# Row-sum reciprocals taken once per half of an attention unit, and two more weight chunks converted ahead of the FFN

## The chip, the cores and the metric

The kernel runs on one core of a Trainium2 chip. The metric is the device time of one execution in microseconds (us). Five engines work side by side, each through its own instructions in order: PE (matmul), DVE (vector), ACT (activations, copies), POOL (GpSimd), and SP, which issues all DMAs here. Before the change the median of three runs is 726.29 us (726.19 to 726.36).

## The reference

An attention with a position bias is followed by a two-layer feed-forward block (FFN). 4 batches, 8 heads, 576 positions, head width 64; FFN width 2048; all in float32.

```python
def _attn_ref(q, k, v, w1, b1, w2):
    scores = scale * np.matmul(q, k.transpose(0, 1, 3, 2))
    psi_rel = np.log1p(np.abs(pos[:, None] - pos[None, :]))
    psi_i = np.log1p(np.maximum(pos[:, None], 1.0))
    bias = np.maximum((psi_rel / psi_i)[..., None] @ w1 + b1, 0.0) @ w2
    scores = scores + bias.transpose(2, 0, 1)[None]
    attn = np.exp(scores - np.max(scores, axis=-1, keepdims=True))
    attn = attn / (np.sum(attn, axis=-1, keepdims=True) + 1e-09)
    return np.matmul(attn, v)

def _moe_ref(x, w_in, w_out):
    h = x @ w_in
    return np.maximum(0.01 * h, h) @ w_out
```

The second function is applied to the first one's result, as 2304 tokens of 512.

## The kernel before, in words

**Three stages follow one another.** First the position bias is made and written to DRAM (`gen_*`, to some 56 us). Then come 16 attention units of one head pair and one batch each. Then the FFN runs over five token blocks (`BLOCKS`: four of 512 and one of 256 tokens).

**A unit** has nine tiles in the order `KINDS`: A0, B0, A1, B1, M, A2, B2, A3, B3. A and B are the two heads, the digit is a group of 128 query rows, and M holds the last 64 rows of both heads. A0 to B1 with half of M make the half g=0, the rest g=1. The main loop calls `step(n)` for each tile number n. One step issues, in this order: the score matmuls of tile n (L230, into one of two PSUM buffers `ps_s`) and its softmax start on DVE (L252: bias added, scaled, row minimum taken); the reciprocal work `recip` of tile n-1 (L265, L266 on DVE, L269 on POOL, which spreads the reciprocals over a 128-wide tile `rb`); what is left of earlier outputs (L360; then `pv_exit`: L344, L345 and L348); the transposes of tile n-3 (`transposes`, L295, L298, L299, L314, L315 on PE, with the copies into the tile `PT` on ACT, L302 and L311, and DVE, L305 and L317); the product with v (`pv`, L335), twice per unit; and last the exponential on ACT (L260). "Step 6" below is the step whose n is six tiles into a unit; pv of half 0 is issued in step 0 of the next unit, pv of half 1 in step 4 of it. A score matmul needs its `ps_s` buffer back, so it waits for the softmax start two tiles earlier.

Every row sum is turned into its reciprocal, spread by POOL, transposed by PE beside the last 64 columns of the probabilities, and copied on into row 9 of `PT`, where `pv_exit` multiplies by it. Units 1, 5, 9 and 13 do more in `pv_exit`: there the tokens of block 0 are also split into a high part and a low rest (L344, L345, L360).

**Work laid between.** In steps 0 and 4, from unit 2 on, the loop pops two operations of `early_ops`: the conversion of the FFN weights. A chunk m has two halves (`wi`, `wo`). Each half takes one ACT operation (`w_abs`, L400), four on DVE (`w_bits`, L407, L409, L411, L413) and then the split into two parts (`w_hi` on ACT, L419; `w_lo` on DVE, L423). In attention the bits of chunks 0 to 4 are made; only chunk 0 is split as well. In the same steps DVE casts the q and k of the next unit (L192, L197), and POOL makes their low parts (L204, L207).

**The FFN's first block** carries the rest of the conversion. It has 16 rows, one for each chunk m: `ffn1` (12 matmuls, L441), the activations on ACT (`ffn_act`, L449 and L450, both out of one buffer), the rest `gl` on DVE (`ffn_lo`, L456) and `ffn2` of the row two before (12 matmuls, L467 to L469). A list `todo` holds the conversion operations with a cost each; `work(budget)` pops them until the budget is used, twice in a row:

```python
                work(2.6)
                ffn_act(n, m)
                work(2.6)
                ffn_lo()
```

So what `todo` puts on ACT and DVE stands ahead of that row's activations and of its `gl`. `ffn2` of row 0 adds up in the two `ps_s` buffers that `ffn1` of rows 0 and 1 filled, so its second half needs the activations of row 1 done. Each engine keeps to the written order.

Of the kernel before, what the change touches and what calls it, by code (L numbers as in the profile page):

```python
# [8 lines left out]
F32 = mybir.dt.float32  # L9
# [26 lines left out]
def attention_ffn(ctx: ExitStack, tc: tile.TileContext, qt, kt, vm, vt, wi, wo, cst, out):  # L36
# [199 lines left out]
    def softmax_a(n):  # L236
        u, kind = tile_id(n)
        hp = u // B
        bt = bias[hp, "M"][:] if kind == "M" else bias[hp, kind[1]][:, 0 if kind[0] == "A" else 1, :]
        col = 1 if kind[0] == "B" else 0  # L240
        if col == 0:
            mx_t[n] = ap.tile([128, 2], F32, tag="mx", name="mx", bufs=6)
            sm_t[n] = ap.tile([128, 4], F32, tag="sm", name="sm", bufs=6)
        else:
            mx_t[n], sm_t[n] = mx_t[n - 1], sm_t[n - 1]
# [8 lines left out]
        ex_q.append((p, i, sm_t[n][:, col:col + 1]))  # L254

# [18 lines left out]
    pv_q = []

    def pt_tile(u, g):
        PT[u, g] = ap.tile([128, 10, HS], F32, tag="PT", name="PT", bufs=2)

    def halves(t):
        return t[:].rearrange("p (a c) -> p a c", a=2)  # L280

    def transposes(n, at):
        u, kind = tile_id(n)
        p = pp.pop(n)
        p0 = S + 64 if kind[0] == "B" else 0
        if kind == "A0":
            pt_tile(u, 0)
            tails[u, 0] = pstile("o")
        elif kind == "M":
            pt_tile(u, 1)  # L290
            pv_ps[u, 0] = pstile("o")
            tails[u, 1] = pstile("o")
# [18 lines left out]
        nc.scalar.copy(out=PT[u, g][:, 0:8, c].rearrange("p (j h) c -> p j h c", h=2)[:, :, h, :], in_=t0[:].rearrange("p (j c) -> p j c", j=4))  # L311
        if h == 1:
            tl = halves(tails[u, g])
            nc.tensor.transpose(tl[:, 0, c], p[:, 512:640], ident[:])  # L314
            nc.tensor.transpose(tl[:, 1, c], rb_t.pop(n)[:], ident[:])  # L315
            if i2 == 1:
                nc.vector.tensor_copy(PT[u, g][:, 8:10, 0:256], tl)  # L317
                if g == 1:
                    pv_q.append((at, u, 1))
# [159 lines left out]
    with tc.manual_schedule():  # L479
# [7 lines left out]
        for n in range(NTILE + LAG + 6):  # L487
# [138 lines left out]
```

## Time and profile before

| what | value |
|---|---|
| median of three runs | 726.29 us |
| the profiled execution | 725.89 us, with a span of 723.7 us from its first to its last instruction |
| PE busy | 703.4 us (97%) |
| DVE busy | 394.2 us (54%) |
| ACT busy | 365.7 us (51%) |
| POOL busy | 127.0 us (18%) |
| mean granted TensorE clock | 1.000 |

A matmul's record overlaps the next one's, so PE's busy share says little. What a stage loses on PE is read from the time between equal points of the work, and from rows that carry a wait in square brackets: its length and who ended it.

### The profile page before, as it was taken

The numbers are of one execution on the slowest core, as the hardware profiler recorded it, in microseconds if no ns is written. First come the engines' busy times: TensorE is split into PE (matmuls) and PEld (weight loads), VectorE is DVE, ScalarE is ACT, GpSimd is POOL, SyncE is SP. The second block draws the span as 40 slices with busy tenths as digits, with TensorE's granted clock in tenths as the row PEclk, the third lists the DMA queues.
The fourth block names the chain that finished last, engine by engine and source line by source line (L and its number), as shares of the span: only waits on it lengthen the run. The fifth ranks groups of instructions, "written<-read, shape, count | busy, mean of one in ns | idle before, by whom it ended". The sixth has DMA issues, their size and how long they took to land.

```text
span 723.7 us, 11398 instructions
## 1 busy us (share of the span) xinstructions
PE 703.4 (97%) x4192; PEld 556.7 (77%) x4192; DVE 394.2 (54%) x1012; ACT 365.7 (51%) x808; POOL 127.0 (18%) x167
## 2 busy tenths in 40 slices
PE   6899999999999999998999999999999999999998
PEld 2347788778877887776777888888888888888996
DVE  7997789789888889759998211112111221112111
ACT  7797777777868677764555231132221231122221
POOL 2104545445544444300000000000000000000000
PEclk9999999999999999999999999999999999999999
DMA  9798848537626960103552010000100010000100
GB/s 222 241 314 244 224 109 242 129 88 216 188 69 164 249 172 18 59 1 120 175 175 83 1 58 1 1 0 1 58 1 1 0 59 1 0 1 0 59 1 30
DMA packets 30263, 68.26 MB, mean 94 GB/s; under 512 B 8192, under 2 KB 8320, under 8 KB 30208
## 3 DMA queue, kind: packets, MB, share of 16 engines
q1 hardware_dynamic: 30208, 67.54, 32.9%
q8 instruction: 33, 0.54, 0.3%
q14 instruction: 22, 0.18, 0.1%
HBM read 51.92 MB, written 15.61 MB: 93 GB/s over the span
## 4 chain that ended last, share of the span: by engine, by line
PE 80%; DVE 16%; issue 1%; DMA 1%; ACT 1%; SPq 0%; DVEq 0%
PE ps_o L441 11%; PE ps_t L441 11%; PE ps_o L335 10%; PE ps_s L230 10%; PE ps_s L469 8%; PE ps_s L467 8%; PE ps_s L468 8%; PE ps_t L295 7%; DVE p L252 2%; PE ps_o L123 2%; DVE tmp L411 2%; PE ps_t L123 2%; DVE tmp L413 2%; DVE r L112 2%; DVE wol L423 1%
## 5 line engine op out<-in xcount | busy, mean ns | idle before, releaser
L456 DVE TENSOR_TENSOR gl<-g,gh 128x512 fp32r<-128x512 f32 (+1 forms) x80 | 51.0, 638 | 263.9 <-ACT g L450 263.9
L230 PE MATMUL ps_s<-ks,qs 128*128 128x288 f32 x640 | 120.2, 314 | 3.1 <-DVE mx L252 3.1
L469 PE MATMUL ps_s<-woh,gl 128*128 128x512 f32 x288 | 112.9, 392 | 1.9 <-DVE gl L456 1.9
L467 PE MATMUL ps_s<-woh,gh 128*128 128x512 f32 x288 | 112.5, 390 | 1.6 <-ACT g L450 1.6
L468 PE MATMUL ps_s<-wol,gh 128*128 128x512 f32 x288 | 112.3, 390 | 0.0
L252 DVE CUSTOM_DVE_ANT_0 p<-ps_s,bias 128x576 f32<-128x576 f32 x128 | 95.0, 751 | 24.3 <-PE ps_s L230 23.6
L260 ACT ACTIVATE p<-p,mx 128x576 f32<-128x576 f32 x128 | 99.9, 780 | 11.3 <-DVE mx L252 10.4
L230 PEld LDWEIGHTS ps_s<-ks,qs 128*128 128x128 f32 x640 | 89.4, 189 | 18.8 <-DVE mx L252 5.0
L311 ACT COPY PT<-ps_t 128x512 f32<-128x512 f32 x128 | 73.7, 576 | 37.5 <-PE ps_t L295 37.5
L449 ACT ACTIVATE gh<-ps_o 128x512 fp32r<-128x512 f32 (+1 forms) x39 | 21.5, 552 | 124.4 <-PE ps_o L441 124.4
L295 PE MATMUL ps_t<-ident,p 128*128 128x128 f32 x512 | 76.9, 273 | 0.9 <-ACT PT L311 0.8
L449 ACT ACTIVATE gh<-ps_t 128x512 fp32r<-128x512 f32 (+1 forms) x39 | 21.5, 552 | 111.1 <-PE ps_t L441 111.0
L335 PE MATMUL ps_o<-PT,v 128*64 128x288 f32 x512 | 69.2, 412 | 0.0
L469 PEld LDWEIGHTS ps_s<-woh,gl 128*128 128x128 f32 x288 | 54.0, 188 | 16.2 <-DVE gl L456 5.0
L467 PEld LDWEIGHTS ps_s<-woh,gh 128*128 128x128 f32 x288 | 54.2, 188 | 12.6 <-ACT g L450 2.0
L295 PEld LDWEIGHTS ps_t<-ident,p 128*128 128x128 f32 x512 | 61.7, 140 | 2.7 <-ACT PT L311 1.8
L468 PEld LDWEIGHTS ps_s<-wol,gh 128*128 128x128 f32 x288 | 54.2, 188 | 10.6
L441 PE MATMUL ps_t<-xh,wil 128*128 128x512 f32 (+1 forms) x156 | 57.3, 367 | 0.0
L441 PE MATMUL ps_o<-xh,wil 128*128 128x512 f32 (+1 forms) x156 | 57.3, 367 | 0.0
L441 PE MATMUL ps_t<-xl,wih 128*128 128x512 f32 (+1 forms) x156 | 57.3, 367 | 0.0
L441 PE MATMUL ps_o<-xl,wih 128*128 128x512 f32 (+1 forms) x156 | 57.3, 367 | 0.0
L441 PE MATMUL ps_o<-xh,wih 128*128 128x512 f32 (+1 forms) x156 | 57.3, 367 | 0.0
(98 smaller groups left out, 1114.5 us busy)
## 6 DMA issues: line engine op xcount, KB each, us to landing
raw<-kt SPq DMA_DIRECT2D x32, 304.0 KB, 5.8
raw<-qt SPq DMA_DIRECT2D x32, 288.0 KB, 5.2
raw<-wi SPq DMA_DIRECT2D x16, 512.0 KB, 3.6
raw<-wo SPq DMA_DIRECT2D x16, 512.0 KB, 3.6
scr<-x SPq DMA_DIRECT2D x21, 295.5 KB, 4.0
bias<-scr SPq DMA_DIRECT2D x16, 288.0 KB, 5.3
out<-x SPq DMA_DIRECT2D x18, 256.0 KB, 2.1
v<-vm SPq DMA_DIRECT2D x16, 256.0 KB, 4.1
```

The source lines that it names most:

```text
L230: nc.tensor.matmul(s_[:, S0 + HS * hh:S0 + HS * hh + HS], qs[:, c0:c0 + 128], ks[:, k0 + HS * hh:k0 + HS * hh + HS], start=(j == 0), stop= ...
L252: nc.vector.tensor_tensor_reduce(out=p, in0=s_[:, S0:S0 + S], in1=bt, scale=-0.125, scalar=3.4e38, op0=ALU.add, op1=ALU.min, accum_out=i)
L260: nc.scalar.activation(out=p, in_=p, func=AF.Exp, bias=i, scale=-1.0, accum_out=sm)
L295: nc.tensor.transpose(t0[:, 128 * jb:128 * jb + 128], p[:, p0 + 128 * jb:p0 + 128 * jb + 128], ident[:])
L311: nc.scalar.copy(out=PT[u, g][:, 0:8, c].rearrange("p (j h) c -> p j h c", h=2)[:, :, h, :], in_=t0[:].rearrange("p (j c) -> p j c", j=4))
L335: nc.tensor.matmul(o[64 * h:64 * h + 64, 0:HS], l, r, start=(jb == 0), stop=(jb == 4))
L441: nc.tensor.matmul(h_[:, :N], w, x[:, :N], start=(j == 0), stop=(j == len(mms) - 1))
L449: nc.scalar.activation(out=gh[:, :N], in_=h_[:, :N], func=AF.Prelu, alpha=0.01)
L456: nc.vector.tensor_sub(gl[:, :N], g[:, :N], gh[:, :N].bitcast(F32))
L467: nc.tensor.matmul(o, gh[:, c], wt[m][2][:], start=(m == 0), stop=False)
L468: nc.tensor.matmul(o, gh[:, c], wt[m][3][:], start=False, stop=False)
L469: nc.tensor.matmul(o, gl[:, c], wt[m][2][:], start=False, stop=(m == MF - 1))
```

## The change

One tile of row sums serves a unit's half: four sums for g=1, five for g=0 with M. `recip` runs after M and after B3 alone, twice a unit instead of five times. POOL spreads four reciprocals over 256 columns in one copy and, after M, a fifth over 128. PE transposes the 256 columns in two pieces (`turn_rb`), in the step of M for half 0 and in that of B3 for half 1; the count of transposes stays. `PT` is one tile for all units, with both halves in it. With that M's copies become one on ACT and two on DVE, which were two and four. The PSUM tile that took the tails takes the product with v as well. Seven chunks' bits (`EARLY`) are made in attention instead of five, three operations at a time instead of two, with four 128x512 buffers for chunks 5 and 6. In the FFN `work` gets 2.1 instead of 2.6.

```diff
+EARLY = 7
+    tmp_x = {(m, i): xp.tile([128, DM], F32, name=f"y{m}{i}") for m in range(5, EARLY) for i in range(2)}
+    PT = ap.tile([128, 2, 10, HS], F32, name="PT")
...
+        g, sc = int(KINDS.index(kind) > 4), 4 if kind == "M" else 2 * (int(kind[1]) % 2) + col
+        if kind in ("A0", "A2"):
+            sm_t[u, g] = ap.tile([128, 12], F32, tag="sm", name="sm", bufs=3)
...
     def recip(n):
-        w = 2 if tile_id(n)[1][0] == "B" else 1
-        sm = sm_t[n]
+        u, kind = tile_id(n)
+        g = int(kind != "M")
+        sm, w = sm_t.pop((u, g)), 4 if g else 5
         nc.vector.tensor_scalar_add(sm[:, 0:w], sm[:, 0:w], 1e-9)
-        nc.vector.reciprocal(sm[:, 2:2 + w], sm[:, 0:w])
-        rb = rb_t[n] = ap.tile([128, 128], F32, tag="rb", name="rb", bufs=3)
-        one = sm[:, 2:2 + w].rearrange("p (h o) -> p h o", o=1).to_broadcast([128, w, 128 // w])
-        nc.gpsimd.tensor_copy(rb[:].rearrange("p (h c) -> p h c", h=w), one)
-        if w == 1:
+        nc.vector.reciprocal(sm[:, 6:6 + w], sm[:, 0:w])
+        rb = rb_t[u, g] = ap.tile([128, 384], F32, tag="rb", name="rb", bufs=2)
+        one = sm[:, 6:10].rearrange("p (h o) -> p h o", o=1).to_broadcast([128, 4, 64])
+        nc.gpsimd.tensor_copy(rb[:, 0:256].rearrange("p (h c) -> p h c", h=4), one)
+        if g == 0:
+            nc.gpsimd.tensor_copy(rb[:, 256:384], sm[:, 10:11].to_broadcast([128, 128]))
             nc.gpsimd.tensor_copy(pp[n][:, S:S + 64], pp[n][:, S - 64:S])
...
+    def turn_rb(u, g, rb):
+        for i in range(2):
+            nc.tensor.transpose(outs[u, g][:, 256 + 128 * i:384 + 128 * i], rb[:, 128 * i:128 * i + 128], ident[:])
+        nc.vector.tensor_copy(PT[:, g, 8:10, 0:256], halves(outs[u, g]))
...
-            for g in range(2):
-                nc.scalar.copy(out=PT[u, g][:, 0:8, 256:288].rearrange("p (j h) c -> p j h c", h=2), in_=src[:, :, :, g, :])
-                for h in range(2):
-                    r = slice(64 * h, 64 * h + 64)
-                    nc.vector.tensor_copy(PT[u, g][r, 8:10, 256:288], halves(tl)[r, :, 64 * h + 32 * g:64 * h + 32 * g + 32])
+            nc.scalar.copy(out=PT[:, :, 0:8, 256:288], in_=t0[:].rearrange("p (j g c) -> p g j c", j=8, g=2))
+            for h in range(2):
+                r, c = slice(64 * h, 64 * h + 64), slice(64 * h, 64 * h + 64)
+                nc.vector.tensor_copy(PT[r, :, 8:10, 256:288], halves(tl)[r, :, c].rearrange("p a (g c) -> p g a c", g=2))
+            turn_rb(u, 0, rb)
             pv_q.append((at, u, 0))
...
-        if 0 <= n - 1 < NTILE and KINDS[(n - 1) % 9][0] != "A":
+        if 0 <= n - 1 < NTILE and KINDS[(n - 1) % 9] in ("M", "B3"):
             recip(n - 1)
...
-                for m in range(5):
+                for m in range(EARLY):
...
-            for _ in range({0: 2, 4: 2}.get(i, 0) if n >= 18 else 0):
+            for _ in range({0: 3, 4: 3}.get(i, 0) if n >= 18 else 0):
...
-        for m in range(2, 5):
+        for m in range(2, EARLY):
             todo += [(0, w_hi, m, i) for i in range(2)] + [(0.69, w_lo, m, i, nc.vector) for i in range(2)]
-        todo.append((0, more))
-        halves_ = [(m, i) for m in range(5, MF) for i in range(2)]
+            if m == 4:
+                todo.append((0, more))
+        halves_ = [(m, i) for m in range(EARLY, MF) for i in range(2)]
...
-                work(2.6)
+                work(2.1)
                 ffn_act(n, m)
-                work(2.6)
+                work(2.1)
...
-    nc = bacc.Bacc("TRN2", target_bir_lowering=False, num_devices=1)
+    nc = bacc.Bacc("TRN2", target_bir_lowering=False, num_devices=1, dynamic_dma_scratch_size=2048)
```

Three places of the instruction order show what moves. The line numbers of the change are a few higher: L258 is the softmax start, L290 the copy of `turn_rb`, L309 the tail copies of M.

DVE in steps 5 to 7 of unit 1, before, from the first piece of `pv_exit` on (`xt`, `x` and `xl` belong to the outputs, `p` and `mx` to the softmax):

```order
L344 TENSOR_TENSOR xt<-ps_o,PT 128x224
L348 TENSOR_TENSOR x_0_69<-ps_o,PT 128x64
L252 ISA p,mx<-ps_s,bias 128x576
L252 ISA mx 128x1
L360 TENSOR_TENSOR xl_927<-xt,xh_926 128x224
L317 COPY PT<-ps_o 128x2x256
L252 ISA p,mx<-ps_s,bias 128x576
L252 ISA mx 128x1
L265 TENSOR_SCALAR sm<-sm 128x2
L266 RECIPROCAL sm<-sm 128x2
L305 COPY PT<-ps_o 64x2x32 x4
```

and now:

```order
L344 TENSOR_TENSOR xt<-ps_o,PT 128x224
L348 TENSOR_TENSOR x_0_69<-ps_o,PT 128x64
L258 ISA p,mx<-ps_s,bias 128x576
L258 ISA mx 128x1
L360 TENSOR_TENSOR xl_912<-xt,xh_911 128x224
L258 ISA p,mx<-ps_s,bias 128x576
L258 ISA mx 128x1
L309 COPY PT<-ps_o 64x2x2x32 x2
L290 COPY PT<-ps_o 128x2x256
```

The large copy moved from ahead of the last softmax start of these to behind the tail copies, which are two instead of four, and the reciprocal pair between them is gone.

POOL over one unit from M's reciprocals on, before (`rb` is the spread reciprocal, `pM` the padded tile of M, `ks` the low part of k):

```order
L271 COPY pM<-pM 128x64
L207 TENSOR_TENSOR ks_996<-raw_79,ks_995 128x576
L269 COPY rb<-sm 128x128
L207 TENSOR_TENSOR ks_996<-raw_79,ks_995 128x640
L269 COPY rb<-sm 128x128
```

and now:

```order
L276 COPY rb<-sm 128x256
L278 COPY rb<-sm 128x128
L279 COPY pM<-pM 128x64
L211 TENSOR_TENSOR ks_980<-raw_83,ks_979 128x576
L211 TENSOR_TENSOR ks_980<-raw_83,ks_979 128x640
L276 COPY rb<-sm 128x256
```

Before `pM` there was one 128-wide copy for M; now a 256-wide one stands ahead of it as well. The two k instructions follow each other with nothing between.

DVE in the FFN's first rows, ahead of row 0's `gl`, before (`wil` and `wol` are low parts of weights, `tmp` is a half under conversion, `gl` ends a row):

```order
L423 TENSOR_TENSOR wil_4463<-tmp,wih_4462 128x512
L423 TENSOR_TENSOR wol_4465<-tmp,woh_4464 128x512
L407 TENSOR_SCALAR tmp<-tmp 128x512
L409 TENSOR_SCALAR tmp<-tmp 128x512
L411 SCALAR_TENSOR_TENSOR tmp<-raw,tmp 128x512
L456 TENSOR_TENSOR gl_4510<-g_4506,gh_4507 128x512
```

and now:

```order
L426 TENSOR_TENSOR wil_4160<-tmp,wih_4159 128x512
L426 TENSOR_TENSOR wol_4162<-tmp,woh_4161 128x512
L426 TENSOR_TENSOR wil_4164<-y_78,wih_4163 128x512
L426 TENSOR_TENSOR wol_4166<-y_79,woh_4165 128x512
L459 TENSOR_TENSOR gl_4207<-g_4203,gh_4204 128x512
```

Since the last output of attention eight low parts (the last two shown) and three bit operations stood ahead of the first `gl`; now it is ten low parts (the last four shown). On ACT, over the same stretch, before:

```order
L450 ACTIVATE g_4506<-ps_s 128x512
L419 CAST wih_4462<-tmp 128x512
L419 CAST woh_4464<-tmp 128x512
L400 ACTIVATE tmp<-raw 128x512 x2
L419 CAST wih_4466<-tmp 128x512
L400 ACTIVATE tmp<-raw 128x512
L449 ACTIVATE gh_4508<-ps_s 128x512
```

and now:

```order
L453 ACTIVATE g_4203<-ps_s 128x512
L422 CAST wih_4159<-tmp 128x512
L422 CAST woh_4161<-tmp 128x512
L422 CAST wih_4163<-y_78 128x512
L422 CAST woh_4165<-y_79 128x512
L422 CAST wih_4167<-y_80 128x512
L422 CAST woh_4169<-y_81 128x512
L403 ACTIVATE tmp<-raw 128x512 x2
L452 ACTIVATE gh_4205<-ps_s 128x512
```

Before, a cast of chunk 5, whose bits DVE had still to make (`wih_4466`), stood ahead of row 1's activations; now every cast there takes a half whose bits were made in attention.

## Rows read from the trace of the kernel before

**Rows 1.** The page's 40 slices: the granted TensorE clock in tenths.

```profile
PEclk9999999999999999999999999999999999999999
```

**Rows 2.** Busy time by stretch (units 1, 2, 5, 9, 13; FFN): length, PE, PEld, DVE, ACT, POOL, PEclk, DMA, GB/s.

```profile
68.27:86.40 18.13, 16.96 (x127) 13.06 (x127) 13.47 (x42) 12.25 (x30) 7.82 (x11) 1.00 0.95 241
86.40:102.26 15.86, 15.86 (x127) 13.04 (x126) 12.66 (x41) 12.77 (x30) 7.83 (x11) 1.00 0.40 97
134.00:151.52 17.52, 16.70 (x128) 13.03 (x127) 14.66 (x44) 13.38 (x32) 8.14 (x11) 1.00 0.35 89
199.12:216.72 17.60, 16.68 (x127) 13.02 (x126) 15.38 (x46) 12.26 (x30) 7.73 (x11) 1.00 0.30 71
264.32:281.63 17.31, 16.69 (x128) 13.02 (x127) 14.21 (x44) 13.39 (x32) 7.85 (x11) 1.00 0.30 72
...
334.38:391.92 57.54, 56.29 (x241) 44.51 (x240) 56.58 (x107) 33.54 (x58) 0.00 (x0) 1.00 0.52 165
```

**Rows 3.** The chain that ended last, undisturbed FFN rows: start, us, what.

```profile
408.40 2.72 PE ps_t L441 x12
413.84 2.72 PE ps_o L441 x12
```

**Rows 4.** DVE in order of time, first FFN block: start, us, engine, line, what.

```profile
335.28 0.68 DVE L456 TENSOR_TENSOR gl<-g,gh 128x512 fp32r<-128x512 f32 x1
...
341.22 0.69 DVE L456 TENSOR_TENSOR gl<-g,gh 128x512 fp32r<-128x512 f32 x1
```

**Rows 5.** PE in order of time, row 0's ffn2 and the next ffn1 (waits in brackets).

```profile
330.09 0.50 PE L469 MATMUL ps_s<-woh,gl 128*128 128x512 f32 x1 [0.61 <-DVE gl L456]
...
332.88 0.50 PE L467 MATMUL ps_s<-woh,gh 128*128 128x512 f32 x1 [1.60 <-ACT g L450]
...
334.38 0.39 PE L441 MATMUL ps_o<-xh,wih 128*128 128x512 f32 x1
```

**Rows 6.** DVE in order of time at the end of attention.

```profile
323.01 0.68 DVE L423 TENSOR_TENSOR wil<-tmp,wih 128x512 fp32r<-128x512 f32 x1
323.61 0.69 DVE L423 TENSOR_TENSOR wol<-tmp,woh 128x512 fp32r<-128x512 f32 x1
```

**Rows 7.** ACT in order of time, the same stretch.

```profile
330.67 0.62 ACT L419 CAST wih<-tmp 128x512 fp32r<-128x512 f32 x1 [4.22 <-DVE tmp L413]
...
332.25 0.58 ACT L450 ACTIVATE g<-ps_s 128x512 f32<-128x512 f32 x1
```

**Rows 8.** DVE in order of time, unit 13, steps 6 and 7.

```profile
277.61 1.22 DVE L360 TENSOR_TENSOR xl<-xt,xh 128x224 fp32r<-128x224 f32 x1
278.75 0.68 DVE L317 COPY PT<-ps_o 128x512 f32<-128x512 f32 x1
279.35 0.74 DVE L252 CUSTOM_DVE_ANT_0 p<-ps_s,bias 128x576 f32<-128x576 f32 x1
```

**Rows 9.** POOL in order of time, unit 13, steps 5 to 7.

```profile
276.73 0.29 POOL L269 COPY rb<-sm 128x128 f32<-128x128 f32 x1 [2.26 <-DVE sm L266]
...
277.16 1.42 POOL L207 TENSOR_TENSOR ks<-raw,ks 128x576 fp32r<-128x576 f32 x1
```

**Rows 10.** PE in order of time, unit 13, the score matmuls behind that.

```profile
280.15 0.80 PE L230 MATMUL ps_s<-ks,qs 128*128 128x288 f32 x4 [0.42 <-DVE mx L252]
```

**Rows 11.** Groups by line and form: count, busy us, mean ns, idle before.

```profile
L269 POOL COPY rb<-sm 128x128 f32<-128x128 f32 x80 | 30.5, 381 | 120.5 <-DVE sm L266 108.9 <-PE ps_t L295 11.6
L265 DVE TENSOR_SCALAR sm<-sm 128x2 f32<-128x2 f32 x64 | 10.8, 169 | 12.4 <-ACT p L260 11.7
```

**Rows 12.** DVE in order of time, an undisturbed unit (12), step 0 into 1.

```profile
250.12 1.37 DVE L411 SCALAR_TENSOR_TENSOR tmp<-raw,tmp 128x512 int32<-128x512 int32 x2
...
252.75 0.08 DVE L252 DVE_READ_ACCUMULATOR2_ANT mx<- 128x1 f32 x1
```

**Rows 13.** PE in order of time, the score matmuls of step 3 there.

```profile
253.20 0.77 PE L230 MATMUL ps_s<-ks,qs 128*128 128x288 f32 x4
```

**Rows 14.** POOL in order of time, unit 0, one spread copy.

```profile
62.57 0.71 POOL L269 COPY rb<-sm 128x128 f32<-128x128 f32 x1 [0.36 <-DVE sm L266]
```

More of the change, by code (lines that the diff above doesn't have):

```diff
@@ L242, in softmax_a @@
             mx_t[n] = ap.tile([128, 2], F32, tag="mx", name="mx", bufs=6)
-            sm_t[n] = ap.tile([128, 4], F32, tag="sm", name="sm", bufs=6)
         else:
-            mx_t[n], sm_t[n] = mx_t[n - 1], sm_t[n - 1]
+            mx_t[n] = mx_t[n - 1]
+        g, sc = int(KINDS.index(kind) > 4), 4 if kind == "M" else 2 * (int(kind[1]) % 2) + col
+        if kind in ("A0", "A2"):
+            sm_t[u, g] = ap.tile([128, 12], F32, tag="sm", name="sm", bufs=3)
         if kind == "M":
@@ L253, in softmax_a @@
         pp[n] = pair[0]
-        ex_q.append((p, i, sm_t[n][:, col:col + 1]))
+        ex_q.append((p, i, sm_t[u, g][:, sc:sc + 1]))
     ex_q = []
@@ L262, in recip @@
     def recip(n):
-        w = 2 if tile_id(n)[1][0] == "B" else 1
-        sm = sm_t[n]
+        u, kind = tile_id(n)
+        g = int(kind != "M")
+        sm, w = sm_t.pop((u, g)), 4 if g else 5
         nc.vector.tensor_scalar_add(sm[:, 0:w], sm[:, 0:w], 1e-9)
-        nc.vector.reciprocal(sm[:, 2:2 + w], sm[:, 0:w])
-        rb = rb_t[n] = ap.tile([128, 128], F32, tag="rb", name="rb", bufs=3)
-        one = sm[:, 2:2 + w].rearrange("p (h o) -> p h o", o=1).to_broadcast([128, w, 128 // w])
-        nc.gpsimd.tensor_copy(rb[:].rearrange("p (h c) -> p h c", h=w), one)
-        if w == 1:
+        nc.vector.reciprocal(sm[:, 6:6 + w], sm[:, 0:w])
[4 more added lines that the diff above has]
+            nc.gpsimd.tensor_copy(rb[:, 256:384], sm[:, 10:11].to_broadcast([128, 128]))
             nc.gpsimd.tensor_copy(pp[n][:, S:S + 64], pp[n][:, S - 64:S])
-    PT, tails, pv_ps = {}, {}, {}
+    outs = {}
     pv_q = []
-    def pt_tile(u, g):
-        PT[u, g] = ap.tile([128, 10, HS], F32, tag="PT", name="PT", bufs=2)
     def halves(t):
         return t[:].rearrange("p (a c) -> p a c", a=2)
+    def turn_rb(u, g, rb):
+        for i in range(2):
+            nc.tensor.transpose(outs[u, g][:, 256 + 128 * i:384 + 128 * i], rb[:, 128 * i:128 * i + 128], ident[:])
+        nc.vector.tensor_copy(PT[:, g, 8:10, 0:256], halves(outs[u, g]))
     def transposes(n, at):
@@ L285, in transposes @@
         p0 = S + 64 if kind[0] == "B" else 0
[L286 to L292, printed above, removed]
+        if kind in ("A0", "M"):
+            outs[u, int(kind == "M")] = pstile("o")
         t0 = pstile("t")
@@ L296, in transposes @@
         if kind == "M":
-            tl = tails[u, 1]
+            rb = rb_t.pop((u, 0))
+            tl = outs[u, 1]
             nc.tensor.transpose(tl[:, 0:128], p[:, 512:640], ident[:])
-            nc.tensor.transpose(tl[:, 256:384], rb_t.pop(n)[:], ident[:])
-            src = t0[:].rearrange("p (j h g c) -> p j h g c", j=4, h=2, g=2)
-            for g in range(2):
-                nc.scalar.copy(out=PT[u, g][:, 0:8, 256:288].rearrange("p (j h) c -> p j h c", h=2), in_=src[:, :, :, g, :])
-                for h in range(2):
-                    r = slice(64 * h, 64 * h + 64)
-                    nc.vector.tensor_copy(PT[u, g][r, 8:10, 256:288], halves(tl)[r, :, 64 * h + 32 * g:64 * h + 32 * g + 32])
+            nc.tensor.transpose(tl[:, 256:384], rb[:, 256:384], ident[:])
+            nc.scalar.copy(out=PT[:, :, 0:8, 256:288], in_=t0[:].rearrange("p (j g c) -> p g j c", j=8, g=2))
[3 more added lines that the diff above has]
+            turn_rb(u, 0, rb)
             pv_q.append((at, u, 0))
@@ L310, in transposes @@
         c = slice(128 * i2, 128 * i2 + 128)
-        nc.scalar.copy(out=PT[u, g][:, 0:8, c].rearrange("p (j h) c -> p j h c", h=2)[:, :, h, :], in_=t0[:].rearrange("p (j c) -> p j c", j=4))
+        nc.scalar.copy(out=PT[:, g, 0:8, c].rearrange("p (j h) c -> p j h c", h=2)[:, :, h, :], in_=t0[:].rearrange("p (j c) -> p j c", j=4))
         if h == 1:
[L313 to L319, printed above, removed]
+            nc.tensor.transpose(outs[u, g][:, c], p[:, 512:640], ident[:])
+            if kind == "B3":
+                turn_rb(u, 1, rb_t.pop((u, 1)))
+                pv_q.append((at, u, 1))
     x_pend, pv_out = [], []
@@ L325, in pv @@
         hp, b = divmod(u, B)
-        if (u, g) not in pv_ps:
-            pv_ps[u, g] = pstile("o")
-        o, pt = pv_ps.pop((u, g)), PT.pop((u, g))
+        o, pt = outs.pop((u, g)), PT[:, g]
         for jb in range(5):
@@ L398, in w_abs @@
     def w_abs(m, i):
-        y = pools["y" if m in (3, 4) else "s"].tile([128, DM], F32, tag="tmp", name="tmp", bufs=4)
+        if (m, i) in tmp_x:
+            y = tmp_x[m, i]
+        else:
+            y = pools["y" if m in (3, 4) else "s"].tile([128, DM], F32, tag="tmp", name="tmp", bufs=4)
         nc.scalar.activation(out=y[:], in_=raws[m, i][:, :, 1].bitcast(F32), func=AF.Abs)
```

## The prediction

> **What bounds the kernel.** I read the 40 slices first: PE's clock is granted in full in every one [rows 1], at its 2.4 GHz level, so nothing here turns on the clock. PE is busy for 97% of the span; that is not yet a limit, so I next cut the span at equal points of the work, from one unit's first product with v to the next unit's. Unit 2 takes 15.86 us with PE busy for 15.86 of it [rows 2]. I cut ten more units that way: each takes 15.86 or 15.87. There PE is the limit, and since the change leaves the number of its matmuls and transposes as it is, these units cannot get shorter. Units 1, 5, 9 and 13 take 18.13, 17.52, 17.60 and 17.31 [rows 2], which is 2.27, 1.66, 1.74 and 1.45 too much.
>
> Then the FFN. An undisturbed row takes 5.44 us, the distance of two ffn1 starts [rows 3]. In the first block, from row 3's ffn1 to row 13's, ten rows take 57.54 us [rows 2] where 54.4 would do: 3.1 us lost. DVE is the reason: it goes from one `gl` to the next in 5.94 us [rows 4] (335.28 to 341.22) with no gap between, two weight halves to a row. Before that, row 0's ffn2 stands twice: 0.61 us for `gl` and 1.60 us for the activations of row 1 [rows 5]. So there are three places where time can be had: the start of the FFN, its first block, and four units.
>
> **The change, part by part.**
>
> *Pace of the first FFN block.* One half costs DVE (5.94 - 0.60) / 2 = 2.67 us, 0.60 being the distance at which such a 128x512 operation follows the one before [rows 6]. By the new order DVE has in rows 1 to 12 the low parts of chunk 6 (2 x 0.60) and 18 halves (18 x 2.67 = 48.1): 49.3 us, or 4.1 a row, and with `gl` 4.7. That is below 5.44, so PE sets the pace: **-3.1 us**. The budget of 2.1 only spreads the work. Where DVE still falls behind in some rows, a third of the loss may stay: -2.0 to -3.1.
>
> *Start of the FFN.* Row 1's activations stood on ACT behind a cast that waited 4.22 us for DVE, because that half's bits were not made yet; the second of the activations ran at 332.25 [rows 7], and PE went on at 332.88 [rows 5]. Now the casts ahead of it take halves that are ready. What is left is `gl` of row 0: the single buffer of the activations ties row 1's second one to it. DVE starts its low parts at 323.01 [rows 6]; ten of them at 0.60 end at 329.0, and `gl` at 329.7. PE can then take its third matmul at about 329.8 (before 330.09). Row 1's second activation follows `gl` by some 0.6 us, at 330.3, before PE needs it (four more matmuls, 0.23 each, end at about 330.9). Then ffn2 ends at 332.1 instead of 334.38 [rows 5]: **-2.3 us**. If ACT still comes late the gain is 0; if `gl` also came on time it would be -2.8. I take -2.3, worked out from the order itself.
>
> *Units 1, 5, 9, 13.* In unit 13, step 6, L360 takes 1.22 us for 224 columns, where the copy behind it takes 0.68 for 512, and it ends 0.25 after POOL's L207 ends [rows 8, 9], as if held by it. Then come the large copy (0.60) and the softmax start, and the score matmuls wait 0.42 us for that [rows 10]. A stop also loses the overlap of neighbouring matmuls: records of 0.39 us [rows 5] stand 2.72 / 12 = 0.23 apart [rows 3], so some 0.2 more. The change takes the copy out of this chain (-0.60), but it puts a 256-wide copy on POOL ahead of L207. One 128-wide copy takes 0.29 us in this place [rows 9], 0.38 in the mean [rows 11]; for the wide one I take 0.35, between once and twice 0.29 (bounds 0.29 and 0.58). L207 and with it L360 end 0.35 later. The softmax start comes 0.25 us earlier, and PE also has two more transposes in this step (0.11 each): the wait of 0.42 nearly goes, with its 0.2. That is -0.6 each. In unit 9 the operations of step 4 shrink as well (two of 0.68 before, now two of 0.35), so about -1.0. In unit 5 step 4 had none on DVE and now gets three of the heavy ones, some 2.0 us, against 0.55 saved by the reciprocals and their wait: 0. In unit 13 it is -0.5. A wait of ACT's in step 2, which the heavier slots of step 0 lengthen a little, costs 0.3 in sum. In all -0.6 - 1.0 - 0 - 0.5 + 0.3 = -1.8.
>
> The Trainium skill ("SBUF — State Buffer", Who interferes with whom) states that a DVE instruction with two SBUF inputs and a GpSimd instruction that reads SBUF block each other for the whole instruction. L360's 1.22 us beside L207 agrees. By that rule what POOL does first decides, which speaks against the wide copy placed ahead of L207.
>
> *Steady units.* Three reciprocal pairs of five leave DVE, 0.28 us each pair, and with them their waits for ACT (11.7 us over all [rows 11]); ACT loses one copy. This has no price here, as PE covers it. The third operation in a slot has to fit: after step 0 the softmax start of step 1 ended at 252.83 [rows 12], and PE wanted it at 253.20 [rows 13], a margin of 0.37. A third heavy operation adds 0.66, but in steps 6 and 7 a pair (0.28) goes and two tail copies stand for four, which brings DVE there some 0.4 earlier. So the three slots of step 0 that hold three heavy ones come out just even; I allow **-0.2** on the gain. The slots of step 4 lie beside a product with v, where DVE idled. Attention in all: -1.8 + 0.2, rounded, **-1.6**, with bounds from -5.5 (all four units down to 15.86, but for unit 1's share that a late load of q explains) to +2.
>
> Sum: -3.1 - 2.3 - 1.6 = -7.0. The profiled execution took 725.89 us, 0.4 below the median of 726.29, so it would take 718.9, and the median **719.3 us**.
>
> **The rivals.**
> - *All disturbances of attention go.* DVE has 1.2 us less of its own work per unit, and the large copy leaves the one chain that stops PE. Against it: unit 5's new bits. Attention then gives -5.2, the FFN -5.4: 715.7.
> - *POOL holds DVE longer.* A copy on POOL has taken 0.71 us [rows 14]; two such ahead of L207 put L360 (0.71 - 0.29) + 0.71 = 1.1 us later, more than the 0.60 taken out, and the four units lose 0.5 each instead of gaining. Attention +2.0: 726.3 - 5.4 + 2.0 = 722.9. Against it: the wide copy comes right behind a short DVE pair, with no two-input operation on DVE beside it. The rule of the Trainium skill cited above ("SBUF — State Buffer", Who interferes with whom) is this rival's.
> - *The start stays as it is*, because a buffer of the activations or a cast of chunk 5 waits for the last reader of attention's memory: only the pace and attention gain: 726.3 - 3.1 - 1.6 = 721.6.
> - *The heavier slots take their time from PE.* All 20 added operations on the path, 16 on DVE with some 0.57 us (2.27 us per half in four) and each of 25 slots with a stop of 0.2: 9.1 + 5.0 = 14.1, against 5.4 in the FFN: 735.0, slower. It decides itself where DVE comes later than the margin of 0.37. Against it: the softmax starts wait for PE, not the reverse, in every undisturbed unit. A third of it (4.7) with the 5.4 of the FFN would end at 725.6, no change.
>
> **How the numbers follow.** Chances: the forecast 0.56 (its own range 717.6 to 721.0), all disturbances gone 0.13, POOL 0.15, the start unchanged 0.07, slots at a third of the price 0.05, at full price 0.04. The range leaves out the two slot cases and about half of the second: **716.2 to 723.0**. What a measurement of this kernel can tell from no change is about 0.2%, 1.5 us. Faster by more than that: 0.56 + 0.13 + 0.15 + 0.07 = 0.91; slower 0.04; within it 0.05.
>
> **What would show it.** In the changed profile ffn1 starts of the first block should lie 5.44 apart from row 3 on, with no wait of PE on `gl`; ffn2 of row 0 should show one wait of about 0.3 us, and none on ACT. Units 1, 9 and 13 should take about 16.8 us or less (unit 1 about 17.5), unit 5 about 17.5, all others 15.86. L207 should start some 0.35 us later behind M's reciprocals. I am wrong if undisturbed units take more than 15.9 us, if the first block's rows still go with DVE, or if ACT waits for DVE ahead of row 1's activations.

## The result

The changed kernel takes 718.51 us in the median of four runs (718.41 to 718.82), the kernel before 726.24 beside it: ratio 0.9894, 95% interval 0.9878 to 0.9909. The forecast was 719.3. The profiled execution took 718.43 us with a span of 716.7; before it was 725.89 and 723.7. Of the 7.46 us between the two, 7.0 lie in the span; what the other 0.4 are is left open.

The page of the changed kernel, busy time of PE and DVE, and the chain that ended last by engine:

```profile
PE 701.1 (98%) x4192; PEld 558.2 (78%) x4192; DVE 382.5 (53%) x884; ACT 363.3 (51%) x792; POOL 115.2 (16%) x135
...
PE 91%; DVE 5%; ACT 2%; issue 1%; DMA 1%; SPq 0%; DVEq 0%
```

Busy time by stretch, units 1, 2, 3, 5, 6, 9, 13 and the ten rows of the first FFN block from row 3 on (columns as in [rows 2], which has units 1, 2, 5, 9, 13 and the block of before):

```profile
68.29:85.91 17.62, 16.73 (x127) 13.10 (x126) 13.93 (x34) 12.00 (x30) 7.07 (x8) 1.00 0.97 248
85.91:102.13 16.22, 16.20 (x128) 13.11 (x127) 12.94 (x37) 13.14 (x31) 6.86 (x8) 1.00 0.29 76
102.13:118.00 15.87, 15.87 (x128) 13.07 (x127) 13.37 (x35) 12.61 (x30) 7.24 (x9) 1.00 0.73 197
133.87:150.69 16.82, 16.51 (x127) 13.10 (x126) 16.27 (x38) 11.75 (x29) 7.19 (x9) 1.00 0.54 153
150.69:166.91 16.22, 16.19 (x128) 13.12 (x127) 12.93 (x37) 13.15 (x31) 6.85 (x8) 1.00 0.34 76
198.65:215.92 17.27, 16.56 (x127) 13.11 (x127) 14.98 (x36) 12.85 (x31) 7.44 (x9) 1.00 0.72 167
263.54:280.36 16.82, 16.51 (x128) 13.09 (x127) 15.48 (x38) 11.69 (x29) 7.20 (x9) 1.00 0.30 77
330.48:384.88 54.40, 54.40 (x241) 45.06 (x240) 52.65 (x99) 31.07 (x55) 0.00 (x0) 1.00 0.45 145
```

The last line is the largest gain: ten rows in 54.40 us with PE busy throughout, against 57.54. Units 1, 5, 9 and 13 are shorter, but units 2 and 6, at 16.22 us, are new among the disturbed ones. PE in order of time, where attention hands over to row 1's ffn1, and around row 0's ffn2:

```profile
320.83 0.50 PE L444 MATMUL ps_s<-xh,wih 128*128 128x512 f32 x1
...
328.08 0.50 PE L472 MATMUL ps_s<-woh,gl 128*128 128x512 f32 x1 [0.29 <-DVE gl L459]
...
330.48 0.39 PE L444 MATMUL ps_o<-xh,wih 128*128 128x512 f32 x1
```

One wait of 0.29 us for `gl` is left of the two in [rows 5], none for ACT. Three stretches, cut at the same points of the work in every kernel, give the account. Attention runs from the first product with v of unit 1 to row 1's ffn1, the start of the FFN from there to row 3's ffn1, and block 0 from there to row 13's ffn1. The table has them in us from the profiled execution of each kernel, together with the experiments of the next section:

| kernel | median us | attention | start | block 0 |
|---|---|---|---|---|
| before | 726.24 | 254.24 | 11.87 | 57.54 |
| changed | 718.51 | 252.54 | 9.65 | 54.40 |
| forecast of the difference | | -1.6 | -2.3 | -3.1 |
| difference | -7.73 | -1.70 | -2.22 | -3.14 |
| e1 bits alone | 724.99 | 258.33 | 9.69 | 54.41 |
| e2 reciprocals alone | 723.01 | 251.51 | 11.93 | 57.45 |
| e3 changed, budget 2.6 | 723.37 | 252.76 | 9.68 | 58.98 |
| e4 abs apart | 717.67 | 251.54 | 9.65 | 54.40 |
| e5 high half late | 718.37 | 252.01 | 9.65 | 54.41 |
| e6 k early on POOL | 720.76 | 254.76 | 9.64 | 54.40 |
| e7 two products last | 718.96 | 252.90 | 9.89 | 54.41 |
| e8 low half on POOL | 717.16 | 251.44 | 9.65 | 54.40 |
| e9 = e5 + e8 | 713.32 | 247.60 | 9.67 | 54.40 |
| e10 `gl` early | 716.91 | 252.46 | 8.30 | 54.40 |
| e11 all | 711.45 | 247.11 | 8.29 | 54.41 |
| e12 e9's edits on before | 720.13 | 248.57 | 11.86 | 57.53 |

The point at which attention's stretch begins lies between 67.7 and 68.7 us in these runs, and each experiment was timed beside the kernel before (medians of 726.26 to 726.68 us there), not beside the changed one. Hence medians a few tenths apart say little, and the stretches say more.

### The profile page after: what moved, and what is told of

The parts are those of the page before. It is cut to its first block, busy times and chain, and to the rows that moved or that the text cites. A ratio compares the mean times of both kernels' runs of the same rounds, so it can differ in the third digit from the quotient of the medians.

```text
span 716.7 us, 11129 instructions
## 1 busy us (share of the span) xinstructions
PE 701.1 (98%) x4192; PEld 558.2 (78%) x4192; DVE 382.5 (53%) x884; ACT 363.3 (51%) x792; POOL 115.2 (16%) x135
## 4 chain that ended last, share of the span: by engine, by line
PE 91%; DVE 5%; ACT 2%; issue 1%; DMA 1%; SPq 0%; DVEq 0%
PE ps_o L444 13%; PE ps_t L444 13%; PE ps_s L234 11%; PE ps_o L335 11%; PE ps_s L472 9%; PE ps_s L470 9%; PE ps_s L471 9%; PE ps_t L300 8%; DVE r L116 2%; PE ps_o L127 2%; PE ps_t L127 2%; PE ps_s L127 1%; PE ps_o L289 1%; PE ps_o L318 1%; DVE p L258 1%
## 5 line engine op out<-in xcount | busy, mean ns | idle before, releaser
L258 DVE CUSTOM_DVE_ANT_0 p<-ps_s,bias 128x576 f32<-128x576 f32 x128 | 94.5, 750 | 24.9 <-PE ps_s L234 24.7
```

## The experiments

The fences below show the edits shortened, with `...` for what is left out. A "slot" is the place in step 0 or 4 where the loop pops conversion operations.

**e1: the bits alone.** On the kernel before, everything of the diff except reciprocals, `PT` and tail copies. The smaller DMA scratch goes along; no run has it by itself.

```
+EARLY = 7
...
-for m in range(5):
+for m in range(EARLY):
...
-{0: 2, 4: 2}
+{0: 3, 4: 3}
...
-work(2.6)      # both places
+work(2.1)
```

> The kernel before with the bits alone: seven chunks, three operations in a slot, budget 2.1; reciprocals and tail copies as before. Theory A (the two halves of the change are independent; the FFN's gain is all the bits' doing, and three-operation slots cost PE only where the first bit operation stands in the slot of its own abs, behind a disturbed unit: units 2, 6 and 9, 0.36 to 0.45 us each): FFN start -2.2, block 0 -3.1, attention +1.2, so 726.2 - 5.3 + 1.2 = 722.1 us; second-unit and sixth-unit length 16.2 instead of 15.86. Theory B (the slots are covered only because the reciprocals left DVE): attention +3 or more, 724 us or above.

724.99 us, ratio 0.9981 (0.9972 to 0.9990): theory B. The FFN gains all of its 5.3 us, and attention gives 4.1 back. Units 2, 3, 6, 7, 11 and 12, undisturbed before, take 16.14 to 16.25, which is 2.0 of it. The larger part, 2.4, lies in units 5, 9 and 13, which grow from 17.52, 17.60 and 17.31 to 18.48, 18.39 and 17.95 (unit 1 is 0.3 shorter). Unit 12, step 0 into 1, DVE in order of time in e1, and the score matmuls of PE that wait for it:

```profile
252.97 1.36 DVE L416 SCALAR_TENSOR_TENSOR y<-raw,y 128x512 int32<-128x512 int32 x2
254.26 0.68 DVE L418 SCALAR_TENSOR_TENSOR y<-raw,y 128x512 int32<-128x512 int32 x1
...
256.21 0.08 DVE L254 DVE_READ_ACCUMULATOR2_ANT mx<- 128x1 f32 x1
...
256.34 0.79 PE L232 MATMUL ps_s<-ks,qs 128*128 128x288 f32 x4
```

and the same place in the changed kernel:

```profile
248.76 1.46 DVE L414 SCALAR_TENSOR_TENSOR y<-raw,y 128x512 int32<-128x512 int32 x2
250.14 0.68 DVE L416 SCALAR_TENSOR_TENSOR y<-raw,y 128x512 int32<-128x512 int32 x1
...
252.09 0.08 DVE L258 DVE_READ_ACCUMULATOR2_ANT mx<- 128x1 f32 x1
...
252.53 0.38 PE L234 MATMUL ps_s<-ks,qs 128*128 128x288 f32 x1
```

Counted from the unit's first product (251.30 and 247.67), the last operation of the softmax start ends at 4.99 us in e1 and at 4.50 in the changed kernel, 0.49 earlier. In the changed kernel that is 0.36 before PE's score matmuls begin (4.86). In the kernel before they begin at 4.75 ([rows 13], first product at 248.45), so 4.99 is 0.24 too late for that order. The unit takes 16.25 us in e1 and 15.87 in the changed kernel: the same three operations cost 0.38 us in one and nothing in the other.

**e2: reciprocals and tail copies alone.** The changed kernel with `EARLY = 5`, two operations in a slot, budget 2.6.

> The changed kernel with five chunks, two operations in a slot and budget 2.6: reciprocals and tail copies alone. Theory A (independent halves): FFN as before (start 11.87 us, block 57.5 us), attention -1.7 as in the changed kernel and another -1.2 that the slots had cost there, so 726.2 - 2.9 = 723.3 us; units 2 and 6 at 15.87, unit 9 at 16.8. Theory B (the loss of units 2, 6 and 9 in the changed kernel comes from the reciprocals for four blocks at once, not from the slots): attention -1.7, 724.5 us, and units 2 and 6 stay at 16.2.

723.01 us, ratio 0.9955 (0.9942 to 0.9967), -2.73 in attention: theory A. Units 2 and 6 take 15.88 and 15.87, unit 9 16.82, unit 5 16.81. The FFN is as before. e1 and e2 together give -4.5 us, the change gives -7.7: the halves are not independent. Without the other half of the change the slots cost 4.1, with it 252.54 - 251.51 = 1.0. No run parts the reciprocals from the tail copies.

**e3: the budget of before.**

```
-work(2.1)
+work(2.6)
```

> The changed kernel with the budget of before, 2.6. Theory A (DVE has 4.7 us of work per row of 5.44, so the budget only spreads it): 718.5 us, ffn1 starts still 5.44 apart from row 3. Rival (the budget is what keeps gl on time): some rows longer than 5.44, 719 to 720 us.

723.37 us: both theories fell, the first altogether and the rival in its size. Row 3 takes 6.07 and rows 4 to 11 take 5.93 or 5.94 each, so block 0 is even longer than before. From row 1 to row 13 the two stretches together take 68.66 us in e3, 69.41 before and 64.05 in the changed kernel: what the start gains, DVE takes back in the block. DVE in order of time, e3:

```profile
333.79 0.69 DVE L459 TENSOR_TENSOR gl<-g,gh 128x512 fp32r<-128x512 f32 x1
...
339.72 0.69 DVE L459 TENSOR_TENSOR gl<-g,gh 128x512 fp32r<-128x512 f32 x1
...
345.65 0.69 DVE L459 TENSOR_TENSOR gl<-g,gh 128x512 fp32r<-128x512 f32 x1
```

the changed kernel:

```profile
332.20 0.69 DVE L459 TENSOR_TENSOR gl<-g,gh 128x512 fp32r<-128x512 f32 x1
...
337.46 0.69 DVE L459 TENSOR_TENSOR gl<-g,gh 128x512 fp32r<-128x512 f32 x1
```

Between two `gl` stand ten conversion operations in e3 (two whole halves, 5.93 us) and eight in the changed kernel, with 5.26 us from `gl` to `gl`. A row of PE takes 5.44. That DVE has work for only 4.7 us a row in the mean helps nothing: the list is emptied at the budget's rate, and DVE is late until it is empty. The opposite case, the smaller budget with five chunks, was not run.

**e4: abs apart from its first bit operation.** A slot ends before a bit operation that would read an abs (`w_abs`, on ACT) issued in the same slot.

```
+if f is w_bits and args[2] == 0 and tuple(args[:2]) in fresh:
+    break
```

> The changed kernel, with a slot ended where its next operation would be the first bit operation of a half whose abs stands in the same slot; seven chunks and up to three operations as before. Theory A (DVE waiting 1.4 to 1.7 us for abs in the slot is what units 2, 6 and 9 pay): units 2 and 6 at 15.87, unit 9 at 16.8, in all -1.2: 717.3 us. Rival (three heavy operations in a slot are too many wherever they stand): 718.5 us within 0.3, the loss moves to other units.

717.67 us, attention -1.00: theory A. Units 2 and 6 take 15.87, unit 9 16.86. Unit 2 in the changed kernel, ACT and then DVE in order of time:

```profile
88.53 1.22 ACT L403 ACTIVATE tmp<-raw 128x512 f32<-128x512 f32 x2
...
89.21 0.43 DVE L410 TENSOR_SCALAR tmp<-tmp 128x512 f32<-128x512 f32 x1 [1.41 <-ACT tmp L403]
89.56 0.75 DVE L196 CAST qs<-raw 128x1152 fp32r<-128x1152 f32 x1
```

The two abs stand behind two Exp and a copy on ACT, DVE waits for the first of them, and the cast of q and the softmax start stand behind that wait on DVE. The same wait (1.42 us) in unit 11 costs nothing: the unit ahead of it was undisturbed, and its abs start 1.91 us into the unit, 0.7 earlier than the 2.62 of unit 2.

**e5: the high half of x at the end of its step.**

```
-nc.scalar.copy(out=hi, in_=x[:, 0:c]); x_pend.append(...)   # in pv_exit
+hi_pend.append(...)                # the copy behind softmax_b
```

> The changed kernel, with ACT's copy of the high half of x (L345) issued at the end of its step, behind the transposes' copy and the Exp, instead of ahead of them. Theory A (what stops the transposes in units 1, 5, 9 and 13 is ACT's L316, queued behind a copy that waits for DVE's multiplication): no wait of T(M) on ACT; each of these four units some 0.5 shorter (0.28 and the lost overlap of 0.2), the first half of unit 1 some 0.8: -2.8, 715.7 us. Rival (L360 on DVE then waits for the later copy, and the score matmuls wait for it in turn): 718.0 us or more, with a wait on L258 in place of that on L316.

718.37 us: the rival, in its mechanism. The changed kernel first, unit 5: ACT, then PE, whose row is that of T(M), the transposes of tile M:

```profile
146.41 0.38 ACT L345 CAST xh<-xt 128x224 fp32r<-128x224 f32 x1 [2.49 <-DVE xt L344]
146.70 0.58 ACT L316 COPY PT<-ps_t 128x512 f32<-128x512 f32 x1
...
147.33 0.66 PE L300 MATMUL ps_t<-ident,pM 128*128 128x128 f32 x4 [0.28 <-ACT PT L316]
```

then e5 there, DVE and PE:

```profile
146.99 1.59 DVE L359 TENSOR_TENSOR xl<-xt,xh 128x224 fp32r<-128x224 f32 x1
148.50 0.74 DVE L258 CUSTOM_DVE_ANT_0 p<-ps_s,bias 128x576 f32<-128x576 f32 x1
...
149.31 0.40 PE L234 MATMUL ps_s<-ks,qs 128*128 128x288 f32 x1 [0.57 <-DVE mx L258]
```

The wait on ACT is gone, and PE stands 0.57 us for the softmax start behind the long low-half subtraction instead. Only 0.5 us of attention is gained, 0.3 of it in the first half of unit 1.

**e6: POOL's first subtraction for k one step earlier.**

```
-4: [(0, "k")], 5: [(1, "k", 0)]
+4: [(0, "k"), (1, "k", 0)]
```

> The changed kernel, with POOL's first subtraction for k (L211, 576 columns) issued in step 4, ahead of the copies of the reciprocals, instead of step 5 behind them. Theory A (L360 takes 1.58 us because it stands beside that subtraction, and 0.3 us of each of the second halves of units 1, 5, 9 and 13 hang on it): L360 of these halves takes under 0.6 us, the four units lose 0.3 each: -1.2, 717.3 us. Rival B (L360 is long for another reason, or PE does not wait for it): 718.5 us. Rival C (the copies of the reciprocals now come too late for their transposes): a wait of the transposes L305 or L289, 719 us or above.

720.76 us: slower, and by none of the three ways. POOL, then DVE, unit 5 of e6, and last L272 at the same place in the changed kernel:

```profile
145.39 1.43 POOL L211 TENSOR_TENSOR ks<-raw,ks 128x576 fp32r<-128x576 f32 x1 [4.92 <-issue]
...
147.90 1.54 POOL L211 TENSOR_TENSOR ks<-raw,ks 128x640 fp32r<-128x640 f32 x1
...
145.85 0.99 DVE L272 TENSOR_SCALAR sm<-sm 128x5 f32<-128x5 f32 x1
...
148.06 1.64 DVE L360 TENSOR_TENSOR xl<-xt,xh 128x224 fp32r<-128x224 f32 x1
...
145.72 0.17 DVE L272 TENSOR_SCALAR sm<-sm 128x5 f32<-128x5 f32 x1
```

The second subtraction took the place of the first beside L360, which stays long at 1.64. And the first now holds an operation on five columns: L272, 0.17 us in the changed kernel, takes 0.99 and ends at 146.84, when POOL's has ended (146.82). All behind it on DVE is late, and T(M) waits for ACT 1.12 us here and 1.50 in unit 9 (0.28 and 0.68 in the changed kernel).

**e7: the late operands' products last, at the start of the FFN.**

```
+if (n, m) == (0, 1): mms = mms[0::3] + mms[1::3] + mms[2::3]
+if (n, m) == (0, 0): ...      # the four products with gl last
```

> The changed kernel, with the four products with the low half of the weights put last in row 1's ffn1, and the four with gl last in row 0's ffn2; nothing else moves. Theory A (what is left at the start of the FFN is two operands that come late, wil by 0.49 and gl by 0.29, each with 0.2 to 0.4 of lost overlap): both waits go, the start takes 8.6 instead of 9.65 us: 717.4 us. Rival (DVE's chain of low halves sets the start, so PE only waits later, at row 1's ffn2 or row 2's): 718.5 us.

718.96 us, start 9.89: the rival. Both waits, 0.49 us for `wil` in row 1's ffn1 and 0.29 for `gl`, go, and PE, then ACT, show the new one:

```profile
329.38 0.50 PE L479 MATMUL ps_s<-woh,gh 128*128 128x512 f32 x1 [1.29 <-ACT g L455]
...
328.73 0.60 ACT L455 ACTIVATE g<-ps_s 128x512 f32<-128x512 f32 x1 [2.82 <-DVE gl L461]
```

ffn2's second accumulator takes the PSUM tile of row 1's ffn1; ACT releases it with row 1's second activation, which writes the single `g` buffer and so waits for row 0's `gl`.

**e8: the low half of x on POOL.**

```
-nc.vector.tensor_sub(lo, x, hi.bitcast(F32))
+nc.gpsimd.tensor_sub(lo, x, hi.bitcast(F32))
```

> The changed kernel, with the subtraction for the low half of x (L360) on POOL instead of DVE; ACT's copy of the high half stays ahead of the transposes' copy. Theory A (L360 stands 1.25 to 1.71 us on DVE beside POOL's subtractions for q and k, and the score matmuls pay 0.3 us of that in each second half of units 1, 5, 9 and 13, besides the 0.28 of T(M)'s wait on ACT): the wait on ACT stays, the halves lose 0.3 each: -1.2, 717.3 us. Rival (PE pays for the wait on ACT only): 718.5 us.

717.16 us, attention -1.1: theory A in the sum, with the wait of 0.28 still there, but not in its parts: the second halves of units 1, 5, 9 and 13 get 0.17 shorter each in place of 0.3, and units 2 and 6 get 0.21 shorter. On POOL the subtraction takes 0.67 to 0.81 us.

**e9: e5 and e8 together.**

> The changed kernel, with both: the copy of the high half at the end of its step and the subtraction for the low half on POOL. Theory A (these two are all that stops PE in units 1, 5, 9 and 13, apart from abs in unit 9; either alone only hands the wait to the other): units 5 and 13 at 15.87, unit 9 at 16.3, unit 1 at 16.3: -4.1, 714.4 us. Rival (a third operand comes late in their place, such as the reciprocals' copies behind a longer POOL queue): 717 us or above.

713.32 us, ratio 0.9818 (0.9802 to 0.9834): theory A, and 1 us better. Busy time by stretch, units 1, 2, 5, 9 and 13:

```profile
68.72:85.36 16.64, 16.21 (x127) 13.13 (x126) 11.86 (x34) 12.13 (x30) 7.69 (x10) 1.00 1.02 261
85.36:101.24 15.88, 15.88 (x128) 13.09 (x127) 12.24 (x35) 12.91 (x31) 7.57 (x9) 1.00 0.33 80
132.98:148.86 15.88, 15.88 (x128) 13.08 (x127) 14.15 (x38) 11.83 (x29) 7.83 (x11) 1.00 0.59 165
196.48:212.35 15.87, 15.87 (x128) 13.07 (x127) 13.02 (x36) 12.86 (x31) 8.08 (x11) 1.00 0.66 181
259.97:275.84 15.87, 15.87 (x127) 13.07 (x126) 13.61 (x38) 11.82 (x29) 7.81 (x11) 1.00 0.32 80
```

Alone the edits are worth 0.5 and 1.1 us of attention, together 4.9. Units 2, 6 and 9 lose nothing although abs stands where it stood: its wait costs something only behind a disturbed stretch.

**e10: `gl` of row 0 behind four low halves instead of ten.**

```
-work(2.1)
+work(2.1 if j else 1.0)        # and none in the second place for j = 0
```

It also has e7's order for row 1's ffn1.

> The changed kernel, with the budget of row 0 of the FFN cut so that gl of row 0 stands behind four low halves on DVE instead of ten, and with the products with the low half of the weights last in row 1's ffn1. Theory A (the chain gl of row 0, ACT's second activation of row 1, and the release of its PSUM tile for ffn2 sets the start; gl comes 3.6 us earlier): the start takes 8.3 instead of 9.65 us, and the first block stays at 5.44 a row: 717.1 us. Rival (the six low halves and the bits that move behind gl make DVE late in rows 2 to 12): rows longer than 5.44, 718.5 us or above.

716.91 us: theory A, start 8.30, rows still 5.44. DVE, then PE:

```profile
323.45 0.69 DVE L461 TENSOR_TENSOR gl<-g,gh 128x512 fp32r<-128x512 f32 x1
...
326.13 0.39 PE L472 MATMUL ps_s<-woh,gh 128*128 128x512 f32 x1
...
328.85 0.39 PE L446 MATMUL ps_o<-xh,wih 128*128 128x512 f32 x1
```

ffn2 takes 2.72 us, without a stop.

**e11: all together.**

> All together: abs apart from its first bit operation, high half at the end of its step, low half on POOL, gl of row 0 early. If the causes are independent: 718.5 - 1.2 - 3.7 - 1.4 = 712.2 us, with every unit but the first at 15.87. If one of them hides another: 713.5 to 715 us.

711.45 us, ratio 0.9794 (0.9778 to 0.9810), 7 us under the changed kernel. That is less than either forecast, and yet one cause hides another. Units 2 to 14 take 15.87 or 15.88, as in e9: abs, worth 1.0 us in e4, has nothing left to give there. Attention's 0.5 under e9 lies in unit 1 (16.15), and there it is the load of q: DVE waits 1.67 us for it here and 2.17 in e9, and its cast of q begins 3.56 and 4.06 us into the unit. Among kernels that are alike there the unit varies in the same way (17.51 us in e10, cast at 3.41; 17.97 in e7, cast at 3.86). The two edits of e9 give 4.9 us where 3.7 was counted for them and 1.2 for abs.

**e12: e9's two edits on the kernel before.**

> The kernel before, with the two edits of the ninth experiment alone (the copy of the high half of x at the end of its step, the subtraction for the low half on POOL); reciprocals, tail copies, bits and budget as before. Theory A (these two operations are what disturbs units 1, 5, 9 and 13, in the kernel before as in the changed one; the copies that the change takes out only shorten the chain): units 5, 9 and 13 at 15.9, unit 1 at 16.5, so -6.4, 719.9 us, twice what the reciprocals and tail copies bring by themselves. Rival (the tail copies on DVE, 0.60 us more in step 6 than in the changed kernel, still make the score matmuls wait): each of the four units keeps 0.5 of its loss, 722 us.

720.13 us, ratio 0.9914 (0.9900 to 0.9928), attention -5.67, between the two but nearer to theory A: units 5, 9 and 13 take 16.12 or 16.13, unit 1 16.53. That is twice what the reciprocals and tail copies bring by themselves (e2). The 0.26 us that units 5, 9 and 13 still lose are not traced further.

## Why the prediction was right, and where it was not

*Pace of the first block: the term right (-3.14 for -3.1), its reason wrong in one step.* "The budget of 2.1 only spreads the work" is refuted by e3: bits without the smaller budget give 58.98, longer than before. The step that failed is the mean, 4.7 us a row, put in place of what stands ahead of one `gl`: ten operations or eight. The forecast of this term came out because the budget, which it took to be without effect, was part of the change; in that it was lucky. That fewer halves are needed as well is argued, not shown: at eight operations a row the list of seven chunks is empty in row 12, and by the same count that of five chunks would still hold four operations behind row 13, where the kernel gives back the buffers of the conversion. How much of the 3.1 us the smaller budget alone would give is open.

*Start: right in each step* (-2.22 for -2.3). Attention's gain shifts it by 1.7; with that, the third matmul was due at 328.1 (328.08) and ffn2's end at 330.4 (330.48). That row 0's `gl` ties row 1's activations was in the prediction; e7 shows that this chain, not the late operands, sets the rest, and e10 what it is worth together with e7's order of row 1's ffn1 (1.35).

*Units.* The sum was right by luck (-1.70 for -1.6), since it is made of misses that cancel. A sign of being wrong that the prediction named came true, undisturbed units above 15.9 us: units 2 and 6 take 16.22.

| | forecast | measured |
|---|---|---|
| unit 1 | -0.6 | -0.51 |
| unit 5 | 0 | -0.70 |
| unit 9 | -1.0 | -0.33 |
| unit 13 | -0.5 | -0.49 |
| units 2 and 6 | 0 | +0.36, +0.35 |
| ACT's wait in step 2, slots of three heavy operations | +0.5 | none seen |
| unit 15 and what follows it up to row 1's ffn1 | 0 | -0.42 |

The chain of step 6 went as told. POOL's subtraction starts 0.78 us after the first copy (146.24 to 147.02), 0.43 before [rows 9]: +0.35, as forecast, and L360 goes from 1.22 [rows 8] to 1.58 us, with the wait of [rows 10] gone. What the prediction did not look at is T(M)'s wait for ACT a step earlier, which grew from 0.16 to 0.28 us in unit 5 (from 0.48 to 0.68 in unit 9); it is the one stop of PE above 0.1 us that is left in unit 5. POOL, then DVE, unit 5 of the changed kernel, steps 2 and 5 to 7:

```profile
137.40 2.79 POOL L208 TENSOR_TENSOR qs<-raw,qs 64x576 fp32r<-64x576 f32 x2 [1.78 <-PE ps_s L234]
...
146.24 0.40 POOL L276 COPY rb<-sm 128x256 f32<-128x256 f32 x1 [6.05 <-DVE sm L273]
...
147.02 3.10 POOL L211 TENSOR_TENSOR ks<-raw,ks 128x576 fp32r<-128x576 f32 x2
...
139.01 1.50 DVE L360 TENSOR_TENSOR xl<-xt,xh 128x288 fp32r<-128x288 f32 x1
...
147.10 1.58 DVE L360 TENSOR_TENSOR xl<-xt,xh 128x224 fp32r<-128x224 f32 x1
```

and unit 5 of the kernel before, DVE, POOL and PE:

```profile
140.85 0.44 DVE L360 TENSOR_TENSOR xl<-xt,xh 128x288 fp32r<-128x288 f32 x1
...
141.53 1.41 POOL L204 TENSOR_TENSOR qs<-raw,qs 64x576 fp32r<-64x576 f32 x1
...
147.73 0.66 PE L295 MATMUL ps_t<-ident,pM 128*128 128x128 f32 x4 [0.16 <-ACT PT L311]
```

What failed in the units: in unit 5 three heavy operations in step 4 were charged with all that the rest gave; they lie beside the product with v, and e2, without them, has the same 16.8. In unit 9 (0.45) and in units 2 and 6 the operand order inside a slot was not looked at: a bit operation right behind its abs (e4). "All others 15.86" was therefore wrong for two, and the slots cost 1.0 us (e2) where 0.2 was allowed. That three heavy operations in step 0 cost nothing was right, and with more room than "just even": in unit 12 DVE ends 0.36 us before PE asks, against 0.37 before, because it comes to them 0.6 us earlier than in e1 (1.09 and 1.67 us into the unit) and PE, with two transposes of `turn_rb` there for one, asks 0.11 later. e1 shows what they cost otherwise, 0.38 us in that unit. The shorter unit 15 (15.34 for 15.87, where PE had waited 0.22 us for DVE's tail copy L305) was not foreseen.

*Rivals.* That POOL holds DVE longer is true, and further than was told: without the reciprocals' copies in POOL's queue the two subtractions for q now run back to back (L208 above) and reach step 2, where L360 took 0.44 us in units 1, 5, 9 and 13 and now takes 1.25 to 1.71. It did not end above the forecast; the copy that left the chain, 0.60 us against L360's later end, is the likely reason, and no run parts the two. The Trainium skill ("SBUF — State Buffer", Who interferes with whom) has the rule that a DVE instruction with two inputs in SBUF and a GpSimd instruction that reads SBUF shut each other out; L360's rows agree. The price of these two operations of x, the high-half copy and the low-half subtraction, was far from known: moving both takes 4.9 us out of the changed kernel's attention (e9) and 5.7 out of that of the kernel before (e12). That all disturbances of attention go (-5.2) did not happen in the changed kernel; e9, whose attention is 6.6 us shorter than before, goes beyond it with these two edits. The heavier slots taking PE's time were the truth of e1's kernel (+4.1), and in this one only to 1.0. That rival was also priced at 2.27 us for the four bit operations of a half, where the prediction's own 2.67 less 0.60 gives 2.07.

## What to carry over

Where an engine's queue is filled from a list, compare what stands ahead of each deadline with the period, and not the mean of the work with the mean of the time. A wait that goes away on one engine is worth only what the next late operand leaves: look for the second (e5, e8, e9) before judging the first. And put an operation that reads another engine's fresh result one place further down, since in this kernel such a wait was free only in a stretch that was on time (e4, e9).

## What the runs showed of the hardware

A DVE operation on 128x5 elements with one input took 0.99 us in place of 0.17 and ended 0.02 us after POOL's subtraction (e6). In e6 six of these operations start while POOL subtracts; they take 0.31 to 1.00 us, and each ends within 0.03 us of POOL's end, whatever its length. The Trainium skill ("SBUF — State Buffer", Who interferes with whom) states that `tensor_scalar` too can enter a mode that takes the port pair shared with GpSimd, when its operands allow it; these rows agree. DVE's softmax start, with one input in PSUM, kept 0.74 to 0.76 us in all 90 rows of the changed kernel that overlap such a subtraction.
